# TensorE's order beside the plain feed-forward chunks: the scheduler's, and the program's

## The chip, the cores and the metric

The kernel runs on one core of one Trainium2 chip. The metric is the device time of one execution in microseconds (us); the median of several runs counts. Engines are named as in the profile: PE is TensorE, DVE is VectorE, ACT is ScalarE, POOL is GpSimd, and SP issues most of the DMAs.

## What is computed

Eight images of 3008 tokens by 256 channels are mixed in the frequency domain, and the result goes through a gated feed-forward network. Cut to what matters:

```python
X = np.fft.rfft(x, axis=1)                       # x: 8 x 3008 x 256
Yr = X.real @ w_r - X.imag @ w_i + b_r
Yi = X.real @ w_i + X.imag @ w_r + b_i
Y = sign(Y) * max(|Y| - 0.01, 0)                 # on Yr and Yi
y = np.fft.irfft(Yr + 1j * Yi, n=3008, axis=1)   # read as 24064 tokens x 256
gate = 1 / (1 + exp(-(y @ w_gate)))              # 256 x 1536
out = (gate * (y @ w_val)) @ w_out               # 1536 x 256
```

## The kernel before

**The FFT.** 3008 is 47 x 64, and the transform is done by matrix products in two stages each way. For one image: row products (`fwd_a`, tile `pa`, line 186) over the 47, 16 of them in 8 steps; forward 64-point products (`fwd_b`, tile `pb`, line 247), 12 steps of eight products of 128 columns; mixing (`mix`, tiles `pm` and `pm3`, line 282), 12 steps of 18 products of 256 columns; inverse 64-point products (`inv_b`, tile `pi`, lines 319 to 321), 12 steps of six products of 256 columns; and column products (`inv_a`, tile `pia`, line 351), 16 blocks of four of 94 columns. Between the stages the image goes through HBM (`zd` and `vd`). Row, forward and column products take their float32 operands as they are: here they are called *unsplit*. Mixing, inverse and feed-forward products take each operand as a high and a low part of a narrower type and run three products for one: they are called *split*.

Between `mix` and `inv_b` of the same step lies a chain on other engines. VectorE adds the bias (`yt`, line 284), forms sums (`ys`, four small ones, lines 288 and 289), and applies the threshold (`yc`, lines 271 and 272); ScalarE rounds it to the high part (`yh`, line 293); VectorE forms the low part (`yl`, line 294). The first product of `inv_b` (line 319) needs `yh`, the second (line 320) `yl`. Likewise VectorE and ScalarE make `xsf`, `xsh` and `xsl` (lines 260 to 265) between `fwd_b` and `mix`.

**The feed-forward network.** The first 4608 tokens are nine *plain chunks* of 512 tokens, each in 12 units, one for every 128 hidden features: `ffn1` (tiles `pg` and `pv`, lines 410 to 412) runs 12 products of 512 columns for gate and value, and `ffn2` (tile `po`, lines 438 to 440) six for the output, two units later (`LAG`). All other tokens come after that in 19 pairs of chunks with block products that save multiplications (lines 661 to 741); those are issued in the order of the program on every engine, and the change does not touch them.

**What runs beside what.** The first image's FFT stands alone at the start. Beside the first plain chunk only its own work and half steps of row products run. Beside the units 12 to 107 the FFT work of the other images is spread, in the groups (1), (2, 3), (4, 5), (6, 7): a list `side` of units, each with a weight (1.7 for a step of row products; 0.9 for a forward step, 2.0 for a mixing and 0.7 for an inverse step, added up in one unit; 0.65 for a block of column products). Each feed-forward unit adds a rate to an account, and side units are taken from the list as long as the account covers their weight. `fft_units` makes the units of a group: unit q of an image does the forward step q, the mixing of step q - 1 and the inverse of step q - 2, so the last unit of an image (q = 13) has an inverse step alone, and the last but one (q = 12) a mixing and an inverse step. Images of a pair alternate. A feed-forward unit also does some work on its own chunk's next operands: loads of `vf`, column products and carried rest (`todo`).

**What sets the order.** Each piece of the program is written down engine by engine. Around the start and in the pairs a `manual_schedule` block keeps the program's order. Beside the plain chunks there is none: a scheduler places the instructions on each engine by what is ready and by priority. In most of its units the twelve products of `ffn1` come first, then the six of `ffn2`, then a forward step, a mixing and an inverse step; row and column products stand between as they come, and where an inverse step isn't ready yet, other products are put ahead of it. The FFT's results on PSUM share three banks (`FFT_BANKS`).

Of the kernel before, what the change touches and what calls it, by code (L numbers as in the profile page):

```python
# [10 lines left out]
F32R = mybir.dt.float32r  # L11
# [14 lines left out]
NPL = 9  # L26
HW = 512
# [3 lines left out]
NCB, NTMP, NHP = 10, 9, 12  # L31
# [78 lines left out]
def tile_fft_mix_ffn(ctx: ExitStack, tc, x, w_r, w_i, b_r, b_i, w_one, w_out, mf, mi, mis, fa, fb, out):  # L110
# [3 lines left out]
    P = 128  # L114
    XR = x.shape[2]
    CT = D // P
    NF = w_one.shape[0]
# [8 lines left out]
    NH = NF // 2  # L126
# [9 lines left out]
    fft = ExitStack()  # L136
# [3 lines left out]
    psfs = ExitStack()  # L140
# [101 lines left out]
    def fwd_b(b, q, m, full):  # L242
        zf = held.pop(("z", b, q))
        pb = bank("pb").rearrange("p (c q k) -> p c q k", c=CT, q=2)
        for i in range(2):
            for ct in range(CT):
                nc.tensor.matmul(pb[:, ct, i], zf[:, i, ct * P:(ct + 1) * P], m[:, i], start=True, stop=True)  # L247
        gap("gap_x", 192)
        xh, xl = (p2.tile([P, CT, 3, 2 * R1], F32R, tag=t, name=t) for t in ("xsh", "xsl"))
        if full:  # L250

            xh, xl = (t.rearrange("p c s k -> p c (s k)").rearrange("p c (q k) -> p c q k", q=2) for t in (xh, xl))
            nc.scalar.copy(xh[:, :, :, 64:], pb)
            sub(xl[:, :, :, 64:], pb, xh[:, :, :, 64:])
            for t in (xh, xl):
                nc.scalar.mul(t[:, :, :, :64], t[:, :, :, 128:], -1.0)
        else:

            xf = p2.tile([P, CT, 3, 2, R1], F32, name="xsf", bufs=1)
            nc.scalar.copy(xf[:, :, 0:2].rearrange("p c t q k -> p c q t k"),  # L260
                           pb.rearrange("p c q (t k) -> p c q t k", t=2))
            nc.vector.tensor_add(xf[:, :, 2], xf[:, :, 0], xf[:, :, 1])
            flat = xf.rearrange("p c s q k -> p c s (q k)")
            nc.scalar.copy(xh, flat)
            sub(xl, flat, xh)
        held["xs", b, q] = xh, xl
# [79 lines left out]
    def inv_a(u):  # L346
        vf = held.pop(("v", u))
        pa = bank("pia")[:, :CT * UT].rearrange("p (c h k) -> p c h k", c=CT, h=2)
        for hh in range(2):
            for ct in range(CT):  # L350
                nc.tensor.matmul(pa[:, ct, hh], vf[:, hh, ct * P:(ct + 1) * P], fb_sb[:, :PT], start=True, stop=True)  # L351
        py = pa.rearrange("p c h k -> p c (h k)")
        lo = u * UT
        n = 0
        if lo < T0:
            c, at = divmod(lo, CW)
            n = min(UT, CW - at)
        if 0 < n < UT and lo + n < T0:
            t = p3.tile([P, 3 * P], F32, name="carry", bufs=1)[:, :CT * UT].rearrange("p (c k) -> p c k", c=CT)[:, :, :UT - n]
            nc.scalar.copy(t, py[:, :, n:])  # L360
            held["carry", c + 1] = t, UT - n
        if n:
            split_y(c, at, n, py[:, :, :n])
        if lo + UT > T0:
            t = result("yf")
            t = t[:, :CT * (UT - n)].rearrange("p (c k) -> p c k", c=CT)
            nc.scalar.copy(t, py[:, :, n:])
            nc.sync.dma_start(yd[:, :, lo + n - T0:lo + UT - T0], t)
# [13 lines left out]
    spare = []  # L382
# [68 lines left out]
    def fft_units(bs, ms):  # L451


        aa = [(b, h) for b in bs for h in range(R1 // 8)]
        units = []

        def step_a(i):
            if i == 0:
                for k in range(min(PRE, len(aa))):
                    load_a(*aa[k])  # L460
            if i + PRE < len(aa):
                load_a(*aa[i + PRE])
            fwd_a(*aa[i])
            store_a(*aa[i])

        def loads(q, b):
            if b == bs[0]:
                if q == 0:
                    ms[0, 0] = load_mf(0)
                if q + 1 < NP:  # L470
                    ms[q + 1, 0] = load_mf(q + 1)
                if 0 <= q - 1 < NP and (q - 1, 1) not in ms:
                    ms[q - 1, 1] = load_mi(q - 1, False)
            if q == 0:
                load_b(b, 0)
            if q + 1 < NP:
                load_b(b, q + 1)

        def step(q, b):
            loads(q, b)  # L480
            if q < NP:
                fwd_b(b, q, ms[q, 0], False)
            if 0 <= q - 1 < NP:
                mix(b, q - 1)
            if 0 <= q - 2 < NP:
                inv_b(b, q - 2, ms[q - 2, 1], False)

        first = [(1.7, lambda i=i: step_a(i)) for i in range(len(aa))]
        for q in range(NP + 2):
            wt = 0.9 * (q < NP) + 2.0 * (0 <= q - 1 < NP) + 0.7 * (0 <= q - 2 < NP)  # L490
            units += [(wt, lambda q=q, b=b: step(q, b)) for b in bs]
        return first, units


    def ffn_units():
        units, todo = [], {}
        seq = [(c, f) for c in range(NPL) for f in range(NF)]

        def own(c):

            return range(-(-c * CW // UT), -(-(c + 1) * CW // UT))

        for c in range(1, NPL):
            at = (c - 1) * NF
            for i, u in enumerate(own(c)):
                todo.setdefault(at + (0, 3, 6)[i], []).append(lambda u=u: load_v(u))
                todo.setdefault(at + (3, 6, 9)[i], []).append(lambda u=u: inv_a(u))
            todo.setdefault(at + 1, []).append(lambda c=c: carry(c))

        def unit(n):  # L510
            c, f = seq[n]
            if n == 0:
                for i, u in enumerate(own(0)):
                    if i == 1:
                        w = w1h[:, 0].rearrange("p i t n -> p (i t n)")
                        keep_warm(bank("warm", "l1", L1_BANKS), w[:, :P], w, WARM_V)
                    inv_a(u)
            ffn1(c, f)
            for t in todo.pop(n, ()):
                t()  # L520
            if n >= LAG and n - LAG < len(seq) - BEHIND:
                ffn2(*seq[n - LAG])
        return [lambda n=n: unit(n) for n in range(len(seq))], own(0), own(NPL - 1)[-1] + 1

# [434 lines left out]
    def inverse(g):  # L961

        us = [u for b in g for u in range(b * H // 2, (b + 1) * H // 2) if u >= u0]
        ahead = min(NVF - 1, len(us))

        def begin():
            for u in us[:ahead]:
                load_v(u)

        def go(i):  # L970
            if i + ahead < len(us):
                load_v(us[i + ahead])
            inv_a(us[i])
        return [(0.0, begin)], [(0.65, lambda i=i: go(i)) for i in range(len(us))]

    def behind(g):

# [16 lines left out]
    n_last = len(behind_last)  # L994
    part = len(ffn) - LAST_GAP
    end = len(ffn) - SIDE_GAP
    rates = [sum(w for w, _ in t) / n for t, n in ((side[:-n_last], part - NF), (behind_last, end - part))]
    acc = 0.0
    p4 = None
    ts = [(fp, i) for fp in range(NH) for i in range(2)]  # L1000
    for j in range(NF, len(ffn)):
        c, f = divmod(j, NF)
        ffn[j]()
        acc += rates[j >= part]
        if ts and c >= 3 and f % 4 == 1:
            make_t(*ts.pop(0))
        while side and (acc >= side[0][0] or j >= (part if len(side) > n_last else end) - 1):
            if len(side) == n_last and j < part:
                break
            acc -= side[0][0]  # L1010
            side.pop(0)[1]()
            if len(side) == n_last:
                fft.close()
                p4 = ctx.enter_context(tc.tile_pool(name="p4", bufs=1, reuse_waits="tile"))
                th, tl = (p4.tile([P, NH, 2, 3, P], F32R, name=t) for t in ("th", "tl"))
                spare += [p4.tile([P, 2, HW], F32R, tag="xop", bufs=NCB, name="spare") for _ in range(BEHIND)]
                prep = list(PREP)
                to_load = list(range(NH))
                acc = 0.0
            if not side:  # L1020
                psfs.close()
                psg = ctx.enter_context(tc.tile_pool(name="psg", bufs=1, space=bass.MemoryType.PSUM, reuse_waits="tile"))
        if p4 and to_load and j % 2:
            load_t(to_load.pop(0))
        if c == NPL - 1:
            if f == 0:
                load_y(0)
            if f % 2:
                load_t1(f // 2)
            if prep and f > 2:  # L1030
                operand(0, prep[0])
                split(0, prep.pop(0), sub)
    while to_load:
        load_t(to_load.pop(0))
    while prep:
# [69 lines left out]
```

## Time and profile before

| what | value |
|---|---|
| time of three runs | 2784.44, 2784.85, 2786.99 us; median 2784.85 |
| the profiled execution | 2783.19 us, its span 2781.3 us |
| busy time: TensorE | 2764.9 us (99%) |
| VectorE, ScalarE, GpSimd | 2080.8 (75%), 1308.5 (47%), 710.5 us (26%) |
| chain that ended last | TensorE 95%, VectorE 3% |
| plain chunks with FFT work beside them | from 183.90 to 1061.10 us of the span |
| mixing products of these, line 282 | 1008 rows, 188.5 us, 286 ns each |

The mean clock granted to TensorE was 1.00 over the span. In the rows of the timeline each line begins with the start of a group of instructions (us) and its length, then engine, line, operation, output and inputs, how many it groups, and in brackets what it waited for. Rows of TensorE overlap, since its products are pipelined: the difference of two starts tells how long the products between took to issue. The rows that carry the argument are shown in the prediction.

### The profile page before, as it was taken

What the parts mean: (1) busy time and instruction counts of PE and PEld (TensorE: products, weight loads), DVE (VectorE), ACT (ScalarE), POOL (GpSimd) and SP (SyncE); (2) the same over time, 40 slices, a digit from 0 to 9 for tenths busy, and PEclk for the clock granted to TensorE, in tenths of its full rate; (3) what the DMA queues carried; (4) which work ended last, traced back from release to release, by engine and by line L of the source; (5) the groups of instructions that cost most, each with busy time, mean ns of one, the idle gap of its engine ahead of it and who ended that gap; (6) DMA issues with size and microseconds to landing.
All of it is one profiled execution on the core that took longest, in us unless ns stands there. A gap on an engine that the chain in (4) does not pass through costs nothing.

```text
span 2781.3 us, 38253 instructions
## 1 busy us (share of the span) xinstructions
PE 2764.9 (99%) x13896; PEld 2302.9 (83%) x13896; DVE 2080.8 (75%) x3109; ACT 1308.5 (47%) x2276; POOL 710.5 (26%) x638
## 2 busy tenths in 40 slices
PE   9999999999999999999999999999999999999999
PEld 6678888888899988888888888888888888888887
DVE  5778788767687536777777777777777777777776
ACT  4664554545455444444444444444444444444443
POOL 0211010224100002333333333333333343333321
PEclk9999999999999999999999999999999999999999
DMA  9876544666554561000000000000000000000000
GB/s 300 268 215 192 171 144 150 200 188 190 169 153 147 177 196 45 31 16 16 31 31 16 16 31 31 31 16 16 31 31 16 16 31 31 28 3 31 31 16 16
DMA packets 173469, 241.01 MB, mean 87 GB/s; under 512 B 14592, under 2 KB 124896, under 8 KB 173280
## 3 DMA queue, kind: packets, MB, share of 16 engines
q1 hardware_dynamic: 163776, 214.93, 25.0%
q0 software_dynamic: 9408, 23.60, 2.6%
q8 instruction: 110, 1.80, 0.3%
q14 instruction: 79, 0.65, 0.1%
q10 hardware_dynamic: 96, 0.04, 0.0%
HBM read 134.17 MB, written 104.33 MB: 86 GB/s over the span
## 4 chain that ended last, share of the span: by engine, by line
PE 95%; DVE 3%; DMA 1%; ACT 1%; issue 0%; SPq 0%; DVEq 0%; ACTq 0%
PE pd L670 11%; PE pc L670 11%; PE pa L670 11%; PE po L647 7%; PE po L645 7%; PE po L646 7%; PE pm L282 5%; PE pb L670 5%; PE pia L351 4%; PE pa L186 3%; PE pb L247 3%; PE pg L410 2%; PE pg L411 2%; PE pg L412 2%; PE pv L410 2%; PE pv L412 2%
## 5 line engine op out<-in xcount | busy, mean ns | idle before, releaser
L645 PE MATMUL po<-hh,w 128*128 128x512 f32 x912 | 354.9, 389 | 0.0
L646 PE MATMUL po<-hh,w 128*128 128x512 f32 x912 | 354.8, 389 | 0.0
L647 PE MATMUL po<-hl,w 128*128 128x512 f32 x912 | 354.8, 389 | 0.0
L729 POOL TENSOR_TENSOR c<-c,c 128x512 f32<-128x512 f32 x114 | 147.8, 1296 | 806.5 <-DVE c L725 609.7
L670 PE MATMUL pc<-s,w1h 128*128 128x512 f32 x912 | 281.1, 389 | 0.0
L670 PE MATMUL pa<-a,w1h 128*128 128x512 f32 x912 | 280.7, 389 | 0.0
L725 DVE TENSOR_TENSOR c<-u,pc 128x512 f32<-128x512 f32 x228 | 156.6, 687 | 97.3 <-PE pc L670 91.4
L700 DVE TENSOR_TENSOR u<-u,pb 128x512 f32<-128x512 f32 x228 | 155.2, 681 | 90.6 <-PE pb L670 61.7
L617 ACT CAST hh<-v 128x512 fp32r<-128x512 f32 x114 | 70.7, 620 | 306.0 <-DVE v L710 306.0
L670 PEld LDWEIGHTS pc<-s,w1h 128*128 128x128 f32 x912 | 171.2, 188 | 36.0
L646 PEld LDWEIGHTS po<-hh,w 128*128 128x128 f32 x912 | 171.2, 188 | 35.8
L647 PEld LDWEIGHTS po<-hl,w 128*128 128x128 f32 x912 | 171.2, 188 | 35.6
L645 PEld LDWEIGHTS po<-hh,w 128*128 128x128 f32 x912 | 171.2, 188 | 35.6
L670 PEld LDWEIGHTS pa<-a,w1h 128*128 128x128 f32 x912 | 171.2, 188 | 35.5
L621 POOL TENSOR_TENSOR hl<-c,hh 128x512 fp32r<-128x512 f32 x114 | 152.4, 1337 | 185.9 <-ACT hh L617 185.9
L282 PE MATMUL pm<-w_sb,xsh 128*128 128x256 f32 x1008 | 188.5, 286 | 1.7 <-ACT xf L187 1.2
L670 PE MATMUL pc<-s,w1l 128*128 128x512 f32 x456 | 177.4, 389 | 0.0
L670 PE MATMUL pa<-a,w1l 128*128 128x512 f32 x456 | 177.4, 389 | 0.0
L702 DVE TENSOR_TENSOR v<-u,pd 128x512 f32<-128x512 f32 x228 | 156.8, 688 | 24.4 <-DVE u L700 0.9
L731 DVE TENSOR_TENSOR u<-u,pd 128x512 f32<-128x512 f32 x228 | 156.6, 687 | 24.5 <-DVE c L725 0.9
L704 DVE TENSOR_TENSOR v<-v,pc 128x512 f32<-128x512 f32 x228 | 156.7, 687 | 24.1 <-DVE v L702 0.5
L696 ACT COPY u<-pa 128x512 f32<-128x512 f32 x228 | 133.9, 587 | 70.2 <-PE pa L670 70.0
(174 smaller groups left out, 6721.4 us busy)
## 6 DMA issues: line engine op xcount, KB each, us to landing
zf<-zd SPq DMA_DIRECT2D x96, 256.0 KB, 3.7
vf<-vd SPq DMA_DIRECT2D x128, 192.0 KB, 3.1
out_dram<-ot SPq DMA_DIRECT2D x93, 256.0 KB, 2.2
vd<-vz SPq DMA_DIRECT2D x84, 256.0 KB, 2.9
ypair<-yd SPq DMA_DIRECT2D x19, 1024.0 KB, 4.9
yd<-yf SPq DMA_DIRECT2D x103, 188.0 KB, 3.1
xf<-in_x_dram SPq DMA_DIRECT2D x48, 384.0 KB, 4.0
zd<-xf SPq DMA_DIRECT2D x44, 384.0 KB, 3.5
```

Of the source, the lines that this page charges most:

```text
L282: nc.tensor.matmul(o, l, r, start=(i == 0), stop=(i == len(mms) - 1))
L621: sub_(hl, h, hh)
L645: nc.tensor.matmul(o, wh, hh, start=(f == 0), stop=False)
L646: nc.tensor.matmul(o, wl, hh, start=False, stop=False)
L647: nc.tensor.matmul(o, wh, hl, start=False, stop=(f == NF - 1))
L670: nc.tensor.matmul(o, l, r, start=not more and l is wh and r is xh, stop=l is wl, skip_group_check=more)
L700: add(u, u, b)
L702: add(v, u, d)
L704: add(v, v, c)
L725: add(c12, u, c)
L729: nc.gpsimd.tensor_mul(c12, g12, c12)
L731: add(u, u, d)
```

## The change

A block `tc.manual_schedule(engines={PE})` now stands around the units 12 to 107. Within it TensorE gets its instructions in the order of the program; the other engines are still ordered by the scheduler. The program is written in another order for it:

- `step` of `fft_units` is cut in two, `forward` (the loads and the forward step) and `mixed` (mixing and inverse step). A side unit is now a weight with two parts, a head and a tail: `forward` and `mixed`; row steps have a head alone.
- The side units that fall to a feed-forward unit are collected before that unit is issued, by the same account. Heads are issued ahead of `ffn1`, tails behind `ffn2`. Blocks of column products of earlier groups (`inverse`) carry `False`: they go to the tails if there are tails already, to the heads otherwise.
- A unit's work on its own chunk's operands comes ahead of `ffn1` now, where it stood behind it.

```diff
-        def step(q, b):
+        def forward(q, b):
             loads(q, b)
             if q < NP:
                 fwd_b(b, q, ms[q, 0], False)
+
+        def mixed(q, b):
             if 0 <= q - 1 < NP:
                 mix(b, q - 1)
             if 0 <= q - 2 < NP:
                 inv_b(b, q - 2, ms[q - 2, 1], False)
 
-        first = [(1.7, lambda i=i: step_a(i)) for i in range(len(aa))]
+        first = [(1.7, lambda i=i: step_a(i), None) for i in range(len(aa))]
...
-            units += [(wt, lambda q=q, b=b: step(q, b)) for b in bs]
+            units += [(wt, lambda q=q, b=b: forward(q, b), lambda q=q, b=b: mixed(q, b)) for b in bs]
...
-        def unit(n):
+        def unit(n, heads=(), tails=()):
             c, f = seq[n]
+            for t in heads:
+                t()
...
+            own_units = todo.pop(n, ())
+            if n >= NF:
+                for t in own_units:
+                    t()
             ffn1(c, f)
-            for t in todo.pop(n, ()):
-                t()
+            if n < NF:
+                for t in own_units:
+                    t()
             if n >= LAG and n - LAG < len(seq) - BEHIND:
                 ffn2(*seq[n - LAG])
...
+            for t in tails:
+                t()
...
+    by_hand = tc.manual_schedule(engines={mybir.EngineType.PE})
+    by_hand.__enter__()
     for j in range(NF, len(ffn)):
         c, f = divmod(j, NF)
-        ffn[j]()
         acc += rates[j >= part]
+        now = []
+        while side and (acc >= side[0][0] or j >= (part if len(side) > n_last else end) - 1):
+            if len(side) == n_last and (j < part or now):
+                break
+            acc -= side[0][0]
+            now.append(side.pop(0))
+        heads, tails = [], []
+        for _, head, tail in now:
+            (tails if tail is False and tails else heads).append(head)
+            if tail:
+                tails.append(tail)
+        ffn[j](heads, tails)
...
+    by_hand.__exit__(None, None, None)
```

What this does to the order is shown at three places. A row of these listings has the line, the operation, the output tile and its inputs with the numbers of their buffers, the shape, and how many equal instructions follow one another. Numbers differ between the kernels, since tiles are numbered as the program makes them.

**First place: the end of the first image beside the chunks** (`pi_2881` before and `pi_2903` after are its last inverse step). TensorE before; `pm_2828` is the mixing whose result that step takes:

```order
L282 MATMUL pm_2828<-w_sb_100,xsh_2738 128x256 x2
...
L319 MATMUL pi_2862<-yh_2775,mi_sb_2730 128x256
...
L186 MATMUL pa_2874<-xf_2433,fa_sb_77 96x512
L186 MATMUL pa_2877<-xf_2433,fa_sb_77 96x512
L410 MATMUL pg_2911<-yth_1180,w1h_105 128x512
...
L412 MATMUL pg_2911<-yth_1180,w1l_106 128x512
L319 MATMUL pi_2881<-yh_2858,mi_sb_2825 128x256
L247 MATMUL pb_2899<-mf_sb_2891,zf_2895 128x128 x2
L320 MATMUL pi_2881<-yl_2859,mi_sb_2825 128x256
```

Between the older inverse step (`pi_2862`) and the last one stand two row products, six feed-forward products and, behind its first product, two forward ones. TensorE after, where `pm_2859` is the mixing:

```order
L282 MATMUL pm_2859<-w_sb_100,xsh_2713 128x256 x2
...
L319 MATMUL pi_2893<-yh_2777,mi_sb_2705 128x256
...
L321 MATMUL pi_2893<-yh_2777,mi_sb_2705 128x256
L319 MATMUL pi_2903<-yh_2889,mi_sb_2791 128x256
L320 MATMUL pi_2903<-yl_2890,mi_sb_2791 128x256
...
L186 MATMUL pa_2915<-xf_2696,fa_sb_77 96x512
L186 MATMUL pa_2918<-xf_2696,fa_sb_77 96x512
L247 MATMUL pb_2930<-mf_sb_2803,zf_2926 128x128 x4
```

The last inverse step stands directly behind the older one, and the row and forward products behind both, as heads of the next unit.

**Second place: two steps of the first image in one feed-forward unit.** TensorE before, with the mixings `pm_2137` and `pm_2200`; `pi_2234` takes the result of the first of them:

```order
L282 MATMUL pm_2137<-w_sb_100,xsh_2018 128x256 x2
...
L319 MATMUL pi_2171<-yh_2055,mi_sb_2008 128x256
...
L247 MATMUL pb_2188<-mf_sb_2118,zf_2123 128x128 x4
L282 MATMUL pm_2200<-w_sb_100,xsh_2130 128x256 x2
...
L410 MATMUL pg_2244<-yth_1180,w1h_105 128x512
L411 MATMUL pg_2244<-ytl_1181,w1h_105 128x512
L412 MATMUL pg_2244<-yth_1180,w1l_106 128x512
L319 MATMUL pi_2234<-yh_2167,mi_sb_2120 128x256
L410 MATMUL pg_2244<-yth_1180,w1h_105 128x512
...
L320 MATMUL pi_2234<-yl_2168,mi_sb_2120 128x256
```

Feed-forward products of the next unit (`pg_2244`) stand ahead of the second inverse step and between its products. After, with `pm_2158` and `pm_2202`, and `pi_2236` on the result of `pm_2158`:

```order
L440 MATMUL po_2033<-hl_1920,w2_107 128x512
L282 MATMUL pm_2158<-w_sb_100,xsh_1991 128x256 x2
...
L319 MATMUL pi_2192<-yh_2070,mi_sb_1981 128x256
...
L282 MATMUL pm_2202<-w_sb_100,xsh_2096 128x256 x2
...
L319 MATMUL pi_2236<-yh_2188,mi_sb_2086 128x256
L320 MATMUL pi_2236<-yl_2189,mi_sb_2086 128x256
...
L186 MATMUL pa_2248<-xf_2000,fa_sb_77 96x512
```

Mixing, inverse, mixing, inverse now follow one another, with nothing between. On VectorE at the same place, before, from the first of the two mixings (`yt_2157`) to the low part `yl_2168` that the second inverse step takes:

```order
L284 TENSOR_TENSOR yt_2157<-pm_2137,bias_sb_101 128x512
L265 TENSOR_TENSOR xsl_2131<-xsf_2132,xsh_2130 128x768
L288 TENSOR_TENSOR ys_2159<-pm3_2138,yt_2157 64x256
...
L262 TENSOR_TENSOR xsf_2195<-xsf_2195 128x2x128
L271 TENSOR_SCALAR yc_2164<-ys_2159 128x512
L272 TENSOR_TENSOR yc_2164<-ys_2159,yc_2164 128x512
L265 TENSOR_TENSOR xsl_2194<-xsf_2195,xsh_2193 128x768
L294 TENSOR_TENSOR yl_2168<-yc_2164,yh_2167 128x512
```

VectorE after, from `yt_2178` to `yl_2189`:

```order
L284 TENSOR_TENSOR yt_2178<-pm_2158,bias_sb_101 128x512
L288 TENSOR_TENSOR ys_2180<-pm3_2159,yt_2178 64x256
L289 TENSOR_TENSOR ys_2180<-yt_2178 64x256
L265 TENSOR_TENSOR xsl_2116<-xsf_2117,xsh_2115 128x768
...
L271 TENSOR_SCALAR yc_2185<-ys_2180 128x512
L284 TENSOR_TENSOR yt_2222<-pm_2202,bias_sb_101 128x512
L272 TENSOR_TENSOR yc_2185<-ys_2180,yc_2185 128x512
L288 TENSOR_TENSOR ys_2224<-pm3_2203,yt_2222 64x256
L289 TENSOR_TENSOR ys_2224<-yt_2222 64x256
L288 TENSOR_TENSOR ys_2224<-pm3_2203,yt_2222 64x256
L294 TENSOR_TENSOR yl_2189<-yc_2185,yh_2188 128x512
```

The low part now stands behind one `xsl` and, from the next mixing, its `yt` (ahead of the second `yc`) and three of its `ys`.

**Third place: the end of a group of two images.** TensorE before; `pi_7874` takes the result of a mixing ahead of these rows, and the blocks `pia` are column products of an earlier group:

```order
L319 MATMUL pi_7836<-yh_7649,mi_sb_7492 128x256
...
L351 MATMUL pia_7848<-fb_sb_104,vf_7709 128x94 x4
L319 MATMUL pi_7856<-yh_7751,mi_sb_7719 128x256
...
L351 MATMUL pia_7866<-fb_sb_104,vf_7765 128x94 x4
L410 MATMUL pg_7916<-yth_5849,w1h_105 128x512
...
L319 MATMUL pi_7874<-yh_7832,mi_sb_7719 128x256
L351 MATMUL pia_7884<-fb_sb_104,vf_7846 128x94 x4
L320 MATMUL pi_7874<-yl_7833,mi_sb_7719 128x256
```

After; `pi_7896` takes the result of `pm_7824`:

```order
L282 MATMUL pm_7824<-w_sb_100,xsh_7574 128x256 x2
...
L319 MATMUL pi_7858<-yh_7638,mi_sb_7467 128x256
...
L351 MATMUL pia_7870<-fb_sb_104,vf_7675 128x94 x4
L319 MATMUL pi_7878<-yh_7753,mi_sb_7685 128x256
...
L351 MATMUL pia_7888<-fb_sb_104,vf_7767 128x94 x4
L319 MATMUL pi_7896<-yh_7854,mi_sb_7685 128x256
L320 MATMUL pi_7896<-yl_7855,mi_sb_7685 128x256
...
L351 MATMUL pia_7906<-fb_sb_104,vf_7868 128x94 x4
L247 MATMUL pb_7922<-mf_sb_7777,zf_7918 128x128 x4
```

The last inverse step of the group now follows its mixing in the same unit, with two blocks of column products and two inverse steps between; before, feed-forward products stood there too.

More of the change, by code (lines that the diff above doesn't have):

```diff
@@ L517, in unit @@
                     inv_a(u)
+            own_units = todo.pop(n, ())
+            if n >= NF:
+                for t in own_units:
+                    t()
             ffn1(c, f)
-            for t in todo.pop(n, ()):
-                t()
+            if n < NF:
+                for t in own_units:
+                    t()
             if n >= LAG and n - LAG < len(seq) - BEHIND:
                 ffn2(*seq[n - LAG])
-        return [lambda n=n: unit(n) for n in range(len(seq))], own(0), own(NPL - 1)[-1] + 1
+            for t in tails:
+                t()
+        return [lambda *parts, n=n: unit(n, *parts) for n in range(len(seq))], own(0), own(NPL - 1)[-1] + 1
     def make_t(fp, i):
@@ L973, in go @@
             inv_a(us[i])
-        return [(0.0, begin)], [(0.65, lambda i=i: go(i)) for i in range(len(us))]
+        return [(0.0, begin, False)], [(0.65, lambda i=i: go(i), False) for i in range(len(us))]
     def behind(g):
@@ L996, in tile_fft_mix_ffn @@
     end = len(ffn) - SIDE_GAP
-    rates = [sum(w for w, _ in t) / n for t, n in ((side[:-n_last], part - NF), (behind_last, end - part))]
+    rates = [sum(u[0] for u in t) / n for t, n in ((side[:-n_last], part - NF), (behind_last, end - part))]
     acc = 0.0
@@ L1000, in tile_fft_mix_ffn @@
     ts = [(fp, i) for fp in range(NH) for i in range(2)]
+    by_hand = tc.manual_schedule(engines={mybir.EngineType.PE})
+    by_hand.__enter__()
     for j in range(NF, len(ffn)):
         c, f = divmod(j, NF)
-        ffn[j]()
         acc += rates[j >= part]
+        now = []
[10 more added lines that the diff above has]
+        ffn[j](heads, tails)
         if ts and c >= 3 and f % 4 == 1:
             make_t(*ts.pop(0))
[L1007 to L1022, printed above, removed]
+        if len(side) == n_last and now:
+            fft.close()
+            p4 = ctx.enter_context(tc.tile_pool(name="p4", bufs=1, reuse_waits="tile"))
+            th, tl = (p4.tile([P, NH, 2, 3, P], F32R, name=t) for t in ("th", "tl"))
+            spare += [p4.tile([P, 2, HW], F32R, tag="xop", bufs=NCB, name="spare") for _ in range(BEHIND)]
+            prep = list(PREP)
+            to_load = list(range(NH))
+            acc = 0.0
+        if not side and now:
+            psfs.close()
+            psg = ctx.enter_context(tc.tile_pool(name="psg", bufs=1, space=bass.MemoryType.PSUM, reuse_waits="tile"))
         if p4 and to_load and j % 2:
```

## The prediction

> **What bounds the kernel now.** I read the page first: the busy times of the engines and the chain that ended last. Then the table by stretches, for the part of the run that the change can touch, and a stretch behind it for comparison.
>
> ```profile
> span 2781.3 us, 38253 instructions
> PE 2764.9 (99%) x13896; PEld 2302.9 (83%) x13896; DVE 2080.8 (75%) x3109; ACT 1308.5 (47%) x2276; POOL 710.5 (26%) x638
> PE 95%; DVE 3%; DMA 1%; ACT 1%; issue 0%; SPq 0%; DVEq 0%; ACTq 0%
> ```
>
> ```profile
> 183.90:1061.10 877.20, 872.54 (x5498) 761.29 (x5497) 619.45 (x1069) 431.13 (x740) 107.45 (x156) 1.00 0.57 171
> 1400.00:1600.00 200.00, 200.00 (x881) 164.75 (x880) 155.57 (x214) 91.10 (x159) 67.88 (x51) 1.00 0.06 22
> ```
>
> The columns of the second fence are the stretch, its length, then busy time of TensorE, of its weight loads, VectorE, ScalarE and GpSimd, the granted clock, and DMA. The plain chunks beside which FFT work is spread run from 183.90 to 1061.10 us. There TensorE is busy 872.54 of 877.20 us: it idles 4.66 us in all. Behind the stretch it is busy 200.00 of 200 us. So this is a kernel bound by TensorE from end to end, and two things follow. The waits that a new order could take away come to 4.66 us at most. A wait that a new order brings is paid in full, since TensorE has no idle time left to make it up. VectorE (619 of 877 us) and ScalarE have room.
>
> Busy time can still hide slow issue, so I look at starts and not at durations, further down. First the waits of TensorE in that stretch (waited for: total, times, longest):
>
> ```profile
> PE pi L319 <- ACT yh L293: 0.6, 2, 0.3
> PE pi L319 <- DVE ys L288: 0.5, 1, 0.5
> PE pi L319 <- PE pia L351: 0.2, 1, 0.2
> ```
>
> These are the inverse 64-point products (pi) waiting for the thresholded result of their mixing: 1.3 of the 4.66 us. They matter because the scheduler had until now put other products in front of them.
>
> **The chain from mixing to inverse.** The next rows show one such chain whole. It is the last mixing step of the first image beside the chunks, the same that the first two order listings of the section on the change show.
>
> ```profile
> 274.03 0.39 PE L282 MATMUL pm<-w_sb,xsh 128*128 128x256 f32 x2
> ...
> 275.59 0.69 DVE L284 TENSOR_TENSOR yt<-pm,bias_sb 128x512 f32<-128x512 f32 x1 [0.98 <-PE pm L282]
> ...
> 276.75 2.14 PE L186 MATMUL pa<-xf,fa_sb 94*96 94x512 f32 x4
> ...
> 278.16 0.43 DVE L271 TENSOR_SCALAR yc<-ys 128x512 f32<-128x512 f32 x1
> ...
> 278.62 0.69 DVE L272 TENSOR_TENSOR yc<-ys,yc 128x512 f32<-128x512 f32 x1
> ...
> 279.41 0.62 ACT L293 CAST yh<-yc 128x512 fp32r<-128x512 f32 x1
> ...
> 280.06 0.69 DVE L294 TENSOR_TENSOR yl<-yc,yh 128x512 fp32r<-128x512 f32 x1 [0.75 <-ACT yh L293]
> 280.11 0.36 PE L319 MATMUL pi<-yh,mi_sb 128*128 128x256 f32 x1
> 280.31 0.61 PE L247 MATMUL pb<-mf_sb,zf 128*128 128x128 f32 x4
> ...
> 280.81 0.39 PE L320 MATMUL pi<-yl,mi_sb 128*128 128x256 f32 x1
> ```
>
> Mixing starts at 274.03. VectorE works on it without a foreign instruction between from 275.59 (yt, four ys, two yc), ScalarE rounds it (yh), VectorE forms the rest (yl). The first inverse product, which needs yh, starts at 280.11, that is 6.08 us after the mixing began; the second, which needs yl, at 280.81, 6.78 us after. Mixing and the older inverse step behind it end on TensorE at 276.75, 2.72 us after the start. The 3.36 us between 276.75 and 280.11 are filled with two row products (pa) and half of a feed-forward gate, the 0.5 us behind 280.31 with forward products (pb).
>
> **Part one: the fill that goes.** In program order the row and forward products of a unit stand ahead of its feed-forward products, and the inverse step directly behind the mixing. In most units this is harmless, since the inverse step belongs to a mixing of an earlier unit. At six places the order of after has both in one unit.
>
> At the end of the first image (rows of listing two) the inverse step stands 2.72 us after the start of its mixing. Its second product would start 0.12 us later, at 2.84, and cannot before 6.78: 3.9 us of idle TensorE. What filled them is still to be run.
>
> At two places the first image takes two steps in one unit (the listings of the second place). Between mixing and its inverse stand one inverse step and one mixing, so the inverse starts 2.72 + 2.1 = 4.8 us after the start of its mixing. The chain is longer here, because VectorE's listing has an xsl between the ys, and the next yt and three ys ahead of yl:
>
> ```profile
> L265 DVE TENSOR_TENSOR xsl<-xsf,xsh 128x768 fp32r<-128x768 f32 x84 | 81.2, 966 | 6.7 <-ACT xsh L264 5.7
> ```
>
> That is 0.97 for xsl, 0.65 for yt and 0.55 for three ys of 0.43 in place of the 0.75 us hop to ScalarE: yl is ready at 6.78 + 2.2 = 8.95 us. The stall is 8.95 - 4.8 - 0.12 = 4.0 us, twice.
>
> At the ends of the three groups of two images, one or two column-product blocks (0.9 us each) and one inverse step (0.7) stand between: the inverse starts at 2.72 + 0.9 + 0.7 = 4.3 us in the first of them and 5.2 in the other two. No foreign instruction is in their chains. Stalls: 6.78 - 4.3 - 0.12 = 2.35 us, and twice 1.45.
>
> Sum: 3.9 + 8.0 + 2.35 + 2.9 = 17.2 us. The 1.3 us of waits of the third fence are at such places already, so 15.9 us is new. Behind a waiting inverse step everything on TensorE queues, row, forward and feed-forward products alike; ScalarE's copy of its result and the store on SP's queue come later, but these are read a unit or more later.
>
> **Part two: issue.** The change also cuts the stretches of unsplit products from 196 to 109 (counted in the order), and mixing now follows feed-forward products instead of forward ones. What that is worth is read from starts:
>
> ```profile
> 470.06 1.05 PE L247 MATMUL pb<-mf_sb,zf 128*128 128x128 f32 x8
> 470.87 0.48 PE L282 MATMUL pm<-w_sb,xsh 128*128 128x256 f32 x2
> ...
> 473.07 0.28 PE L319 MATMUL pi<-yh,mi_sb 128*128 128x256 f32 x1
> ...
> 476.61 0.40 PE L410 MATMUL pg<-yth,w1h 128*128 128x512 f32 x1
> ...
> 479.34 1.02 PE L351 MATMUL pia<-fb_sb,vf 96*128 96x94 f32 x8
> ...
> 481.62 0.39 PE L282 MATMUL pm<-w_sb,xsh 128*128 128x256 f32 x2
> ...
> 483.65 0.28 PE L319 MATMUL pi<-yh,mi_sb 128*128 128x256 f32 x1
> ...
> 489.80 1.88 PE L186 MATMUL pa<-xf,fa_sb 94*96 94x512 f32 x4
> 491.11 0.80 PE L410 MATMUL pv<-yth,w1h 128*128 128x512 f32 x1
> 491.75 0.40 PE L411 MATMUL pv<-ytl,w1h 128*128 128x512 f32 x1
> ...
> 504.02 1.03 PE L351 MATMUL pia<-fb_sb,vf 96*128 96x94 f32 x8
> 504.89 1.08 PE L247 MATMUL pb<-mf_sb,zf 128*128 128x128 f32 x8
> 505.73 0.48 PE L282 MATMUL pm<-w_sb,xsh 128*128 128x256 f32 x2
> ```
>
> ```profile
> 733.10 0.48 PE L410 MATMUL pg<-yth,w1h 128*128 128x512 f32 x1
> ...
> 735.92 0.39 PE L438 MATMUL po<-hh,w 128*128 128x512 f32 x1
> ...
> 737.28 0.40 PE L282 MATMUL pm<-w_sb,xsh 128*128 128x256 f32 x2
> ...
> 739.40 0.28 PE L319 MATMUL pi<-yh,mi_sb 128*128 128x256 f32 x1
> ```
>
> Old arrangement: mixing behind forward products 470.87 to 473.07, 2.20 us; twelve feed-forward products behind the inverse step 476.61 to 479.34, 2.73 us; together 4.93. New arrangement, as it stands by chance at 733.10: twelve feed-forward products behind unsplit ones 2.82 us, mixing behind feed-forward 737.28 to 739.40, 2.12 us; together 4.94. So moving the mixing gains nothing there. At 481.62 mixing took 2.03 us, 0.09 less, but only six products stood since the last unsplit ones. If every mixing step ran so, 84 steps would gain 84 x (0.09 + 0.02 for its inverse) = 9 us. I take the case at 733.10, which is the new order product for product, and keep 9 us as the bound. Merging stretches: alone, eight column products take 0.81 us and eight forward ones 0.81 (470.06 to 470.87), and each adds about 0.09 to what follows (2.20 against 2.12): 1.80. Joined they take 0.87 + 0.84 and one 0.09: the same 1.80. I take 1 us of gain for 87 stretches, bounds 0 and 3.
>
> The other 3.4 us of idle time I leave as they are: the row and forward products now stand behind mixing and inverse, when two of the three banks were just written, which can add a wait as easily as remove one.
>
> **Sum.** Of the profiled execution: 2783.19 us (span 2781.3 and 1.9 around it) + 15.9 - 1 = 2798.1. The median of the runs of before, 2784.85, lies 1.7 above that execution, so the forecast is 2799 us, 0.5% slower. A difference of 0.2%, 5.6 us, is about what a measurement of this kernel can tell from none.
>
> **Rivals.** First: mixing runs as at 481.62 and one or two waits are shorter than I have them. Then 15.9 - 9 - 2 = 5 us remain: 2790. For it: three of the four mixing steps that follow feed-forward products run so; against it, the one with the full unit ahead does not.
>
> Second, and on the other side: changing between unsplit and split products costs more than the starts show, and 87 changes fewer pay for all six stalls. The row at 491.11 speaks for it by its duration, 0.80 against 0.40. The starts speak against it: four row products and the first split one behind them take 491.75 - 489.80 = 1.95 us, of which the split one has 0.23, so a row product has (1.95 - 0.23) / 4 = 0.43, change included: 0.25 more would not fit in. It decides from (15.9 + 5.6) / 87 = 0.25 us each; at 0.4 us, 87 x 0.4 = 35, the time would be 2784.85 + 15.9 - 35 = 2766.
>
> Third: the clock. [...]
>
> ```profile
> 1.46 5.34 PE L847 MATMUL warm<-zero 128*128 128x512 f32 x13 [1.46 <-DVE ebias L855]
> 6.63 20.07 PE L186 MATMUL pa<-xf,fa_sb 94*96 94x512 f32 x46
> ```
>
> 13 products of 512 columns in 6.63 - 1.46 = 5.17 us, 0.40 each against 0.23 later (476.61 to 479.34, twelve): 2.2 us lost. If the three longest stalls, of up to 3.4 us before their first product, each cost that, the time is 2799 + 6.6 = 2806. [...]
>
> Fourth: waits for banks at the heads of the units, 0.1 us in most of 84: 2799 + 6 = 2805.
>
> **How the numbers follow.** The six stalls as worked out: 0.60, range of its own 2790 to 2806. First rival 0.18, second 0.10, third 0.06, fourth 0.06. Left out of 2786 to 2810 are the second rival, a part of the first and some of what lies above, 0.18. Faster: the second, 0.10. Within 0.2% (2779.3 to 2790.4): two thirds of the first rival and a sliver of the main case, 0.14. Slower: 0.76.
>
> **What would show it.** Right: TensorE's waits on yh and yl or the DVE rows that stand for it rise to some 15 us over six places, two near 3.9 in the first 90 us of the stretch and one at the first image's end; busy time of the stretch unchanged within 3 us. Wrong: no wait over 2 us at these places, or busy time lower by 9 us or more with mixing at 2.03 us throughout.

## The result, and the profile after

| | median | runs |
|---|---|---|
| before | 2784.93 us | 4, 2784.44 to 2786.99 |
| after | 2831.36 us | 4, 2829.87 to 2834.32 |

The ratio is 1.0167 (95% interval 1.0149 to 1.0184): the change makes the kernel 46 us slower. The forecast was 2799 us in a range from 2786 to 2810. Its direction was right, its size a third of what came: 14 us of 46. In three of the experiments below one execution lay far above the others (3049, 7596 and 11777 us); the ratios leave it out, and the medians, which are over all executions, move by 0.4 us at most for it.

The profiled execution took 2829.87 us. The top of its page:

```profile
span 2828.1 us, 38250 instructions
PE 2785.1 (98%) x13896; PEld 2315.1 (82%) x13896; DVE 2084.9 (74%) x3109; ACT 1304.6 (46%) x2276; POOL 707.3 (25%) x638
PE 92%; DVE 4%; DMA 2%; ACT 1%; issue 1%; SPq 0%; DVEq 0%; ACTq 0%
```

TensorE has the same 13896 products, is busy 20 us longer and idle 27 us longer. The mean clock granted to it is 0.996, where it was 1.00. All of it lies beside the plain chunks. The table by stretches, from the same point as before to the first product of the pairs, which now starts at 1107.70 in place of 1061.10 us, and a stretch behind it:

```profile
183.90:1107.70 923.80, 893.83 (x5500) 774.80 (x5499) 623.37 (x1070) 428.04 (x740) 104.68 (x156) 0.99 0.54 163
1400.00:1600.00 200.00, 200.00 (x880) 164.58 (x879) 156.32 (x215) 88.90 (x155) 67.01 (x50) 1.00 0.06 22
```

TensorE idles 29.97 of 923.80 us (before: 4.66 of 877.20). The waits in that stretch (total, times, longest):

```profile
PE pi L319 <- ACT yh L293: 10.1, 6, 3.0
PE pia L351 <- ACT vz L323: 3.4, 5, 0.7
PE pi L320 <- DVE yl L294: 2.8, 5, 0.9
PE pia L351 <- DVE yt L284: 2.7, 2, 1.8
PE pm L282 <- ACT vz L323: 2.7, 4, 0.7
PE pa L186 <- ACT vz L323: 2.2, 4, 0.6
PE pia L351 <- DMA vf<-vd: 1.7, 1, 1.7
PE pa L186 <- DVE ys L288: 1.2, 3, 0.8
PE pi L319 <- DVE yt L284: 1.2, 1, 1.2
PE pb L247 <- DVE yt L284: 0.6, 1, 0.6
```

The first and third rows are the six inverse steps that the prediction named. The others are new, and nearly all of one kind: products that open a bank wait for the engine that still reads it. `vz` is ScalarE's copy of an inverse step out of its bank, `yt` and `ys` are VectorE's reading of a mixing. With 0.4 us of a row not shown they come to 14.4 us.

How such waits look, and what lies behind the longest ones, shows the timeline of TensorE. First the place of the second listing (two steps of the first image in one unit); the mixing behind whose result `pi` waits started at 214.71, and its inverse step follows at 222.30:

```profile
219.53 0.28 PE L282 MATMUL pm<-w_sb,xsl 128*128 128x256 f32 x1
222.30 0.38 PE L319 MATMUL pi<-yh,mi_sb 128*128 128x256 f32 x1 [2.49 <-ACT yh L293]
223.57 0.39 PE L320 MATMUL pi<-yl,mi_sb 128*128 128x256 f32 x1 [0.89 <-DVE yl L294]
...
224.25 3.58 PE L186 MATMUL pa<-xf,fa_sb 94*96 94x512 f32 x4
227.62 1.91 PE L247 MATMUL pb<-mf_sb,zf 128*128 128x128 f32 x8
```

By starts, 222.30 - 219.53 and 223.57 - 222.30, less the 0.12 us of a product each (the 18 of a mixing step take 2.12 us), the stall is 2.65 + 1.15 = 3.8 us. What comes behind is slow as well: four row products take 227.62 - 224.25 = 3.37 us, 0.84 each, where the prediction worked out 0.43 from the rows of before. The table by stretches of 5 us says why; the third number from the right is the granted clock:

```profile
220.00:225.00 5.00, 1.81 (x7) 1.11 (x8) 4.81 (x10) 1.17 (x2) 1.00 (x2) 0.93 0.37 99
225.00:230.00 5.00, 5.00 (x14) 3.17 (x13) 1.07 (x2) 2.19 (x5) 1.13 (x2) 0.50 0.72 197
230.00:235.00 5.00, 5.00 (x23) 4.11 (x23) 2.50 (x4) 2.27 (x4) 0.00 (x0) 0.89 0.79 247
...
995.00:1000.00 5.00, 5.00 (x20) 4.09 (x20) 0.00 (x0) 1.07 (x2) 0.00 (x0) 0.66 0.84 223
```

Behind the stall TensorE runs at a clock down to 0.50, for (0.07 + 0.50 + 0.11) x 5 = 3.4 us of lost time. Over the whole stretch nine such windows are below 0.99, from 220 to 1000 us; together they lose 11.9 us. Eight of them, 10.2 us, stand behind the first four stalls. The last, at 995 us and 1.7 us, comes some 3 us after the short sixth stall, directly behind a wait for a load:

```profile
994.63 1.10 PE L351 MATMUL pia<-fb_sb,vf 96*128 96x94 f32 x8 [1.74 <-DMA vf<-vd]
```

Then a wait for a bank, at the second of two steps of a pair in one unit:

```profile
347.50 0.28 PE L321 MATMUL pi<-yh,mi_sb 128*128 128x256 f32 x1
347.81 0.58 ACT L323 COPY vz<-pi 128x512 f32<-128x512 f32 x1 [0.26 <-PE pi L321]
348.45 0.51 PE L282 MATMUL pm<-w_sb,xsh 128*128 128x256 f32 x2 [0.67 <-ACT vz L323]
348.74 0.43 DVE L288 TENSOR_TENSOR ys<-pm,yt 64x256 f32<-64x256 f32 x1
348.75 0.59 ACT L260 COPY xsf<-pb 128x512 f32<-128x512 f32 x1 [0.35 <-DVE xsl L265]
```

ScalarE copies the inverse step's result from 347.81 to 348.39; mixing starts at 348.45, 0.8 us behind the end of the inverse step's issue. The last two rows show why no other of the three banks is free: `pm3` of the mixing before is still to be read by VectorE (the row at 348.74 names it `pm`), and the unit's second forward step, issued ahead of the gate, is still to be copied by ScalarE, since `xsf` has one buffer and waits for `xsl` of the first (348.75). So the next mixing needs the bank that was just written. Where no forward result waits this long, the same order brings no such wait: at the place of the second listing the second mixing follows the inverse step without a wait, at 217.53 behind 217.41. Before, no product in this stretch has a row of waiting for `vz`.

### The profile page after: what moved, and what is told of

It is laid out like the page before. It is cut to its first block, busy times and chain, and to the rows that moved or that the text cites. A ratio compares the mean times of both kernels' runs of the same rounds, so it can differ in the third digit from the quotient of the medians.

```text
span 2828.1 us, 38250 instructions
## 1 busy us (share of the span) xinstructions
PE 2785.1 (98%) x13896; PEld 2315.1 (82%) x13896; DVE 2084.9 (74%) x3109; ACT 1304.6 (46%) x2276; POOL 707.3 (25%) x638
## 4 chain that ended last, share of the span: by engine, by line
PE 92%; DVE 4%; DMA 2%; ACT 1%; issue 1%; SPq 0%; DVEq 0%; ACTq 0%
PE pd L681 11%; PE pc L681 11%; PE pa L681 11%; PE po L656 7%; PE po L658 7%; PE po L657 7%; PE pb L681 5%; PE pm L282 5%; PE pia L351 4%; PE pa L186 3%; PE pb L247 3%; PE pg L410 2%; PE pg L412 2%; PE pg L411 2%; PE pv L410 2%; PE pv L412 2%
## 5 line engine op out<-in xcount | busy, mean ns | idle before, releaser
L282 PE MATMUL pm<-w_sb,xsh 128*128 128x256 f32 x1008 | 182.2, 280 | 2.7 <-ACT vz L323 2.7
L282 PEld LDWEIGHTS pm<-w_sb,xsh 128*128 128x128 f32 x1008 | 159.0, 188 | 9.0 <-ACT vz L323 3.5
```

The source lines that it names most:

```text
L282: nc.tensor.matmul(o, l, r, start=(i == 0), stop=(i == len(mms) - 1))
```

## The experiments

Eleven kernels were run. The theory was that three causes add up: (1) six stalls of inverse steps, 15.8 us by the starts of the trace after; (2) the low clock behind them, 11.9 us by its records; (3) waits for one of three banks, 14.4 us by its rows. Against it stood that the low clock or the bank waits were only other faces of the same lateness, or that the fixed order was itself slower.

**One step of an image in a unit.** A side unit is not taken if the feed-forward unit already has a step of the same image; the inverse step then shares no unit with its own mixing.

```diff
+            if any(u[3:] and u[3:] == side[0][3:] for u in now):
+                break
             acc -= side[0][0]
             now.append(side.pop(0))
```

> The changed kernel, but a feed-forward unit takes at most one step of the same image, so that no inverse step stands in one unit with its own mixing. Theory 1 (three causes add up: 15.8 us of stalls of six inverse steps, 11.9 us of low clock behind them, 14 us of waits for banks): the stalls go and with them nearly all of the low clock, 2831 - 15.8 - 10 = 2805 us, mean clock 1.00, bank waits still there. Theory 2 (the low clock has another cause than the stalls): 2831 - 15.8 = 2815 us, mean clock still 0.996. Theory 3 (the stalls were only where some other lateness shows): within 5 us of 2831.

Measured: 2813.52 us (2811.95 to 2816.66), ratio to before 1.0103 (1.0088 to 1.0118). No wait on `yh` or `yl` is left, and of the low clock only 1.7 us, in one window. That contradicts the third theory, and the second for the clock, though the second's time, 2815, is the nearest. The window left is behind a wait of 2.45 us for a load of `vf`, not behind a stall. But 8 us less came off than the first had it. The waits of the stretch:

```profile
PE pia L351 <- ACT vz L323: 4.1, 6, 0.7
PE pm L282 <- ACT vz L323: 3.4, 5, 0.7
PE pia L351 <- DMA vf<-vd: 3.3, 2, 2.5
PE pia L351 <- DVE yt L284: 3.2, 3, 1.8
PE pb L247 <- ACT vz L323: 1.7, 3, 0.6
```

Steps that moved met the same three banks elsewhere: the waits for banks rose from 14.4 to some 18 us, those for loads of `vf` from 1.7 to 3.3.

**Tails between the two kinds of feed-forward products.**

```diff
-            if n >= LAG and n - LAG < len(seq) - BEHIND:
-                ffn2(*seq[n - LAG])
             for t in tails:
                 t()
+            if n >= LAG and n - LAG < len(seq) - BEHIND:
+                ffn2(*seq[n - LAG])
```

> The changed kernel, but the tails (mixing and inverse steps) stand between the 12 and the 6 feed-forward products of a unit, so that six products of 1.36 us lie between an inverse step and the next unit's heads. Theory 1: the heads' waits for banks (10.1 us in all: 3.4 and 2.2 on the copy vz, 4.5 on yt and ys) go but for 0.5, the waits of mixing for banks (2.7 us) and the six stalls stay: 2831 - 9.6 = 2821.5 us. Rival (these waits are covers for lateness that comes back behind them, in the gate products or in the stalls): 2829 to 2833.

Measured: 2843.90 us (2842.78 to 2845.71), 12.5 us slower than the changed kernel. Both theories failed. The waits of row and forward products for banks are gone, 4.0 us, as expected; those of `pia` did not go, since these blocks are tails themselves. But others grew, and the low clock with them, from 11.9 to 15.4 us:

```profile
PE pi L319 <- ACT yh L293: 13.6, 6, 3.7
PE pi L319 <- DVE yt L284: 8.7, 9, 2.8
```

The timeline at one of the nine shows what the six products had been good for:

```profile
481.24 0.40 PE L282 MATMUL pm<-w_sb,xsh 128*128 128x256 f32 x2
...
481.51 0.69 DVE L418 TENSOR_TENSOR sg<-sg,pv 128x512 f32<-128x512 f32 x1 [1.06 <-PE pv L412]
...
482.89 0.69 DVE L427 TENSOR_TENSOR hl<-sg,hh 128x512 fp32r<-128x512 f32 x1 [0.69 <-ACT hh L426]
...
483.50 0.68 DVE L284 TENSOR_TENSOR yt<-pm,bias_sb 128x512 f32<-128x512 f32 x1
...
484.24 0.39 PE L319 MATMUL pi<-yh,mi_sb 128*128 128x256 f32 x1 [0.72 <-DVE yt L284]
```

Mixing now comes directly behind the gate's products, and so VectorE has the gate's own work first: `sg`, then `hl`, which waits for ScalarE. `yt` ends 2.94 us after the mixing began, and TensorE waits for it. In the changed kernel, where these six products stand between, `pi` waits 1.2 us for `yt` in all, once.

**Products without use in the stalls.** The inverse step that waits gets products ahead of it, into the bank that it then overwrites. They add work to the kernel that its output does not need.

```diff
+        if not full and mixed_in[b, q] == now_at[0] and fills:
+            w = w1h[:, 0].rearrange("p i t n -> p (i t n)")
+            keep_warm(pi, w[:, :P], w, fills.pop(0))   # 15, 15, 15, 8, 4, 4
```

> The changed kernel, with 15, 15, 15, 8, 4 and 4 products without use (512 columns each, 0.23 us) ahead of the six inverse steps that wait, into the bank that the step then overwrites: TensorE waits as long as before, but is not idle. Theory 1 (idle gaps lower the clock and that costs 11.9 us): mean clock 1.00 and 2831 - 11.9 + up to 2 = 2819 to 2822 us. Theory 2 (the low clock is not from the gaps, or costs nothing): 2831 us, up to 2833, clock below 1 at the same places.

Measured: 2821.32 us (2820.70 to 2821.92): 10.0 us faster than the changed kernel by 61 more products. The place of the first stall, by the timeline (line numbers are five to one higher in this kernel, 863 are the fill) and in the table by stretches:

```profile
219.39 3.57 PE L863 MATMUL pi<-w1h 128*128 128x512 f32 x15
222.80 0.28 PE L324 MATMUL pi<-yh,mi_sb 128*128 128x256 f32 x1
...
224.03 1.88 PE L187 MATMUL pa<-xf,fa_sb 94*96 94x512 f32 x4
225.75 1.06 PE L248 MATMUL pb<-mf_sb,zf 128*128 128x128 f32 x8
```

```profile
225.00:230.00 5.00, 5.00 (x26) 3.92 (x25) 2.25 (x4) 3.46 (x6) 0.91 (x2) 1.00 0.84 219
```

The inverse step still starts 3.4 us late, since the fill starts at 219.39 and the step at 222.80, but the four row products behind it take 225.75 - 224.03 = 1.72 us in place of 3.37. One window of low clock is left, 1.7 us, again behind the wait for the load (1.72 us at 985.49). So the low clock behind the stalls, 10.2 us by the records, comes from the idle gaps: with them filled the time falls by 10.0 us.

**The old text in fixed order.** Before, with the block that keeps TensorE's program order and nothing else.

```diff
+    by_hand = tc.manual_schedule(engines={mybir.EngineType.PE})
+    by_hand.__enter__()
     for j in range(NF, len(ffn)):
...
+    by_hand.__exit__(None, None, None)
```

> The kernel of before with TensorE in program order beside the plain chunks, without heads and tails: a unit is 12 and 6 feed-forward products, then forward, mixing and inverse steps. Theory 1: inverse steps that stand too close to their mixing again (5.84, 5.84, 4.56, 4.42, 5.31 and 5.31 us behind its start by the order, in place of 4.95, 4.95, 2.83, 4.42, 5.31, 5.31): some 12 us of stalls and 3 to 5 us of low clock, but few bank waits, since the 12 gate products stand behind the inverse step: 2785 - 3 + 12 + 4 = 2798 us. Rival (program order as such costs what the changed kernel lost): 2820 us or more.

Measured: 2797.87 us (2796.61 to 2798.42), ratio 1.0044 (1.0029 to 1.0059). Its waits:

```profile
PE pi L319 <- ACT yh L293: 5.1, 6, 1.2
PE pi L320 <- DVE yl L294: 2.2, 6, 0.4
```

These 7.3 us and 3.4 us of low clock are most of the 13; no row on `vz` stands beside them. The fixed order costs through the steps that stand too close to their mixing, not as such.

**The new text in free order.** The changed kernel without that block.

```diff
-    by_hand = tc.manual_schedule(engines={mybir.EngineType.PE})
-    by_hand.__enter__()
...
-    by_hand.__exit__(None, None, None)
```

> The changed kernel's text (heads ahead of the gate products, tails behind the six others, own column products ahead), but without the block that makes TensorE keep the program's order. Theory 1 (the fixed order is what costs: the scheduler puts gate products ahead of the inverse steps that aren't ready, 5.8 to 7.0 us behind the start of their mixing by the order in place of 2.8 to 5.3): 2788 us, 2783 to 2795, mean clock 0.999 or 1.00. Rival (the new places of the steps cost by themselves, through banks): 2805 us or more.

Measured: 2799.49 us (2798.22 to 2803.89), between the two theories' times, so that neither holds. The scheduler avoids the stalls, 0.9 us of waits on `yh` are left. But the new places bring waits of their own, 6.0 us on `yt` and 2.3 on `hh` ahead of products that open a bank, and 5.2 us of low clock behind two of those on `yt`, of 1.86 and 1.83 us. So heads and tails cost some 15 us without the fixed order, the fixed order 13 without heads and tails, and both together 46: the two do not simply add up.

**The old text in fixed order, one step of an image in a unit.** Both edits as above.

> The text of before in program order on TensorE, as in the run of the old text, and at most one step of the same image in a unit. Theory 1: program order costs nothing once no inverse step shares a unit with its mixing and 12 gate products follow each inverse step: the old text's 2797.9 less 7.3 us of waits on yh and yl and 1.7 of low clock: 2789 us, up to 2792 if a part comes back elsewhere. Rival (moved steps collide elsewhere, as the 8 us that were missing with one step in a unit of the changed kernel): 2797 us.

Measured: 2786.57 us, ratio 1.0006 (0.9996 to 1.0015): no difference from before that these runs can tell, and at most some 4 us by the interval. The clock stayed at 1.00 over the stretch. Program order costs no more than that where the steps are apart and gate products stand behind each inverse step.

**Four banks.** The FFT gets a fourth bank from gate and value, which then have two; in the pairs the third result of a half goes to a bank that the FFT has left.

```diff
-FFT_BANKS, L1_BANKS, L2_BANKS = 3, 3, 2
+FFT_BANKS, L1_BANKS, L2_BANKS = 4, 2, 2
...
-        banks[k] = [bank(t, "l1", L1_BANKS)[:, :HW] for t in ("pa1", "pb1", "pc1")] + [
-            psg.tile([P, 512], F32, tag="l1d", bufs=1, name="pd1")[:, :HW]]
+        banks[k] = [bank(t, "l1", L1_BANKS)[:, :HW] for t in ("pa1", "pb1")] + [
+            psg.tile([P, 512], F32, tag=t, bufs=1, name=n)[:, :HW] for t, n in (("l1c", "pc1"), ("l1d", "pd1"))]
```

In the changed kernel:

> The changed kernel with four banks for the FFT in place of three, and two for gate and value in place of three (the pairs keep theirs). Theory 1 (14.4 us of the loss are waits for one of three banks): most of these waits go, the six stalls and the low clock stay: 2831 - 12 = 2819 us. Rival (the waits are VectorE's and ScalarE's lateness, whichever bank): 2829 to 2833. A second rival (two banks for gate and value are too few): over 2835.

Measured: 2807.37 us, ratio to before 1.0078 (1.0058 to 1.0098), 24.0 us faster than the changed kernel with three and twice what the first theory had. Its low clock is 13.7 us by its records, 1.8 more than with three banks. In the kernel of before, as a control:

> The kernel of before with four banks for the FFT and two for gate and value, as a control of the four-bank run: both theories expect no change, 2782 to 2788 us, since before has 1 to 2 us of waits for banks; over 2790 if two banks for gate and value cost by themselves.

Measured: 2779.17 us, ratio 0.9979 (0.9970 to 0.9989): 5.5 us faster, which no theory had. The waits in the changed kernel with four banks:

```profile
PE pi L319 <- ACT yh L293: 10.6, 6, 3.0
PE pia L351 <- DMA vf<-vd: 3.3, 2, 1.8
PE pi L320 <- DVE yl L294: 2.8, 5, 0.9
PE pm L282 <- DVE yt L284: 0.7, 1, 0.7
```

The stalls stay (10.6 and 2.8 us in place of 10.1 and 2.8), and of the waits for banks 0.7 us are left. They were a cause of their own. Beyond what before gains as well, three banks cost the change 24.0 - 5.5 = 18.5 us. That is a difference of four medians, and the runs of the changed kernel scatter by 4.5 us, so it holds to a few us. It is more than the 14.4 of the rows, because a row begins at the end of the product ahead and not at the end of its issue: the wait at 348.45 is 0.67 by its row and 348.45 - 347.50 - 0.12 = 0.83 by starts. By starts the same 21 waits come to 17.8 us, and ten shorter ones ahead of inverse steps, as the 0.23 us ahead of the one at 346.82, have no row and add 2.6.

**Both cures, and the causes one by one.** The changed kernel with one step of an image in a unit and four banks:

> The changed kernel with both cures: at most one step of the same image in a unit, and four banks for the FFT. Theory 1 (stalls, low clock and bank waits are all of the loss, and the 8 us that came back with one step in a unit were bank waits): 2807.4 (four banks alone) less 15.8 of stalls less 13.7 of low clock: 2778 us, up to 2781 if waits for column-product loads stay; that is below before (2784.7). Rival (a part comes back in other waits again, as it did with three banks): 2786 us or more.

Measured: 2780.60 us, ratio 0.9989 (0.9980 to 0.9998). The loss is gone. With four banks and the products without use:

> The changed kernel with four banks and with the products without use ahead of the six waiting inverse steps. Theory 1 (causes add up): 2807.4 less 13.7 of low clock, plus up to 2: 2794 to 2796 us, mean clock 1.00, so 15.8 us above the kernel with both cures. Rival (with four banks the low clock costs little, since other waits hid it): 2802 us or more.

Measured: 2796.45 us (2794.28 to 2797.50), within 0.5 us of what the first theory had: 10.9 us below the run with four banks alone, for the clock, and 15.9 us above the one with both cures, for the stalls. The old text in fixed order with both cures:

> The text of before in program order, one step of the same image in a unit, four banks. Theory 1: 2786.6 less the 5.5 us that four banks gave the kernel of before: 2781 us, 2779 to 2783. Against the changed kernel with both cures it tells what heads and tails are worth without stalls and bank waits: 3 us less there if mixing behind feed-forward products is what gains (0.08 us for each of 84 steps by the starts in the changed kernel), no difference if merging and moving are worth nothing, as the prediction had it.

Measured: 2776.68 us (2775.38 to 2779.24), ratio 0.9972 (0.9962 to 0.9983). It is the fastest of all, 8 us below before, and 3.9 below the changed kernel with both cures, where the expectation had that one ahead or level. In the profiled execution of the latter, which took 2784.66 us, one wait of 3.85 us for a load of `vf` stands out, behind which five gate products start 0.43 us apart in place of 0.23:

```profile
990.65 1.50 PE L351 MATMUL pia<-fb_sb,vf 96*128 96x94 f32 x8 [3.85 <-DMA vf<-vd]
```

The waits for these loads come to 4.9 us in its profile and to 0.8 in that of the old text.

## Why the prediction was too small

**The six stalls** were right in place and size. By starts, with the products' own 0.12 us taken off, they took 3.80, 3.79 and 3.80 us (worked out: 4.0, 4.0, 3.9), and 2.16, 1.11 and 1.16 (2.35, 1.45, 1.45): 15.8 in place of 17.2 us. The pair of runs with four banks, stalls filled and stalls removed, gives 15.9.

**Issue** was about right. Mixing behind feed-forward products runs as the rows at 733.10 of before had it; the median over 72 such steps of the changed kernel is 2.12 us from the first start to the next product's, and the group of line 282 is at 280 ns:

```profile
L282 PE MATMUL pm<-w_sb,xsh 128*128 128x256 f32 x1008 | 182.2, 280 | 2.7 <-ACT vz L323 2.7
...
608.18 0.48 PE L410 MATMUL pg<-yth,w1h 128*128 128x512 f32 x1
...
611.00 0.39 PE L438 MATMUL po<-hh,w 128*128 128x512 f32 x1
```

Before it was 188.5 us and 286 ns. The twelve gate products behind unsplit ones take 611.00 - 608.18 = 2.82 us, as worked out. No gain from merging shows: with both cures the changed text isn't faster than the old one. The last addition of the forecast, 2798.1 + 1.7, is 2799.8 and not 2799, which changes nothing here.

**The step that failed first** is "The other 3.4 us of idle time I leave as they are: the row and forward products now stand behind mixing and inverse, when two of the three banks were just written, which can add a wait as easily as remove one." It names the mechanism and then prices it at nothing; the fourth rival gave it 0.1 us in most of 84 units, 6 us, and a chance of 0.06. The runs show 18.5 us. Part of the price could be read beforehand: the copy `vz` ends 0.8 us behind the issue of the inverse step (347.62 to 348.39), and what follows that step in the new order, a mixing, a head or a column block, opens a bank at once. What the listings don't show is which results still hold the other two banks, and that decides: the pair in the listing of the second place ran without a wait, the pair at 348.45, with a forward result still uncopied, did not.

**The second** is the low clock, the third rival. It was priced at three gaps of 2.2 us and given a chance of 0.06, and nothing in before shows a ground for so low a chance: the longest wait of TensorE there is the 1.46 us ahead of its first products. In the changed kernel the clock fell to 0.50 (225 to 230 us) behind 2.49 + 0.89 us with a product between, and in the new text in free order to 0.66 (420 to 425 us) behind one gap of 1.86. Measured it cost 10.0 us with three banks and 10.9 with four. The 2.2 us were read from the first products of the run, for which the record of before has a granted clock of 1.00; no run shows them as the cost of a low clock. Behind the first stall 3.4 us were lost, and 10.2 behind the first four.

**The third** is the form of the sum. The rivals "clock" and "banks" stood as alternatives to the main case, each with its own time, though both are added to the stalls: by the prediction's own prices, 2799 + 6.6 + 6 = 2812 us was a possible case, and none of the range's ends took it in.

Together: 15.9 (stalls) + 10.0 (clock) + 18.5 (banks beyond what before has) = 44.4, of 46.4 us. What remains, 2.0 us, is no more than these sizes are uncertain by. On one side stand the wait of 1.7 us for a load and the 1.7 us of low clock behind it, on the other the 1.3 us of stalls that before had and the gain in mixing; no run separates them.

## What to carry to other kernels

Where the scheduler put other instructions between a result and its reader, it also covered the bank that the result leaves; the change paid 15.9 us where the first was lost and 18.5 us where the second was. Whoever fixes the order has to count both distances at every place, from mixing to inverse and from the last product in a bank to the next that opens it, and for the second, which results of earlier steps still hold a bank. TensorE was busy 872.54 of 877.20 us here, and the three effects of the edit, each as its runs gave it, add up to 44.4 of the 46.4 us; where nothing excludes that, a forecast should add them. Two cheap probes separated them here: products without use in a gap (same wait, no idle time) for the clock, 10.0 us, and one more bank for the waits on banks, 24.0 us.

## What the runs showed of the hardware that was not expected

- In the changed kernel gaps of 1.4 to 3 us in the middle of the run were followed by a lower clock, down to 0.50 in a window of 5 us. A place with 0.35, 1.40 and 0.34 us of waits within 3 us, the fourth of the six stalls, was followed by a stretch of 5 us at 0.66; in the new text in free order one gap of 1.86 us was followed by 5 us at 0.66 too. Other gaps as long had nothing behind them, as the wait of 1.84 us for a bank at 726 us in the changed kernel (1.00 from 725 to 740 us), and what tells the two apart is not shown.
- In the changed kernel the drop at 520 us lost 1.7 us (5 us at 0.66), the one at 220 us 3.4 us (three windows at 0.93, 0.50 and 0.89).
- Two banks for gate and value beside the plain chunks cost less than the fourth bank for the FFT gained: together they made the kernel of before 5.5 us faster. Its idle time in the stretch fell from 4.66 us to 2.30 of 874.50; where the other half came from stays open.

```profile
183.90:1058.40 874.50, 872.20 (x5510) 764.18 (x5509) 622.74 (x1070) 431.14 (x741) 107.49 (x157) 1.00 0.57 172
```
